# Linear attention into a sine-gated feed-forward, one core: attention outputs as four 64x64 PE tiles, w_in in natural row order, and a reordered opening

## The chip, the cores and the metric

The kernel runs on one core of one Trainium2 chip. A core has TensorE (PE, matmuls; its weight loads are PEld), VectorE (DVE), ScalarE (ACT), GpSimd (POOL) and SyncE (SP, which issues the DMAs here). All times are microseconds (us) on the device unless marked ns; less is better. The number that is compared is the median time of one execution.

## The reference

Inputs are float32. q, k and v are 8 batches x 8 heads x 576 positions x 64.

```python
q_s = softmax(q, axis=-1)            # over the 64 features of one position
k_s = softmax(k, axis=2)             # over the 576 positions
kv  = einsum('bhsd,bhse->bhde', k_s, v)      # 64x64 for each batch and head
x   = einsum('bhsd,bhde->bhse', q_s, kv)     # then (b s) rows of (h e) = 4608 x 512
h   = x @ w_in                               # 4608 x 2048
g   = h + sin(alpha * h)**2 / (alpha + 1e-9)
out = g @ w_out                              # 4608 x 512
```

## The kernel before

The order on every engine is the order in which the code is written; the framework adds the semaphores. Work falls into an attention part for each batch b (0 to 7) and a feed-forward part for each token tile t (0 to 8) of 512 tokens. Tile t needs the attention of batches up to t, so batch t+1 is worked on inside tile t.

**Attention of one batch.** `load` brings q, k and v into staging tiles (pool `stage`, six buffers that weights share). `exp_q` and `exp_k` (ACT, lines 121) write `qe` and `ke`. `norm_q` sums over features on DVE (line 149), takes the reciprocal and multiplies (line 151; from batch 2 on as one POOL instruction of 128x2304). `cast_v` (line 135, POOL) writes v as bf16 into `vb`, beside a column of ones. `kv_mm` (line 160) makes k-exp times [v, 1] in `kvp`: 36 matmuls of 64x130, two row halves in turn. `kv_norm` divides by the sum and writes two 64x64 blocks into the diagonal of a zeroed 128x128 tile `kvb`. `q_transpose` (line 186) makes three groups of six 128x128 transposes into `tp`, copied to `qT`. `attn_out` (line 195) makes eight matmuls with `kvb` as weights, 256 or 320 columns each, copied to `xT` (line 198).

**Feed-forward of one tile.** For ni = 0 to 15, `mm_h` (line 208) makes four matmuls into one of four `hp` buffers; `sine` (lines 214 to 220) takes the sine on ACT into one of three `s` buffers and squares it on ACT, POOL or DVE as a letter string says (`SQ0` in tiles 0 and 1, ACT from tile 2 on); `combine` (line 224, DVE) writes g. `mm_o` (line 228) makes g times w_out. In tiles t >= 2 the 64 `mm_o` of tile t-1 are spread between the `mm_h` by a count `want`: 20 right after ni = 0, then two or three for each ni. Tile 0's `mm_o` run as one block behind tile 0; its four results are evacuated by `evac_o` (line 233) through three `o` buffers and stored by SP.

**Where the attention stands inside a tile.** At ni = 0: exp_q, exp_k, norm_q, cast_v, then the loads of the next batch. At ni = 4: `kv_mm` and `kv_norm`; at ni = 6 to 8 the transposes; at ni = 9 to 12 `attn_out`. All of it is written ahead of that ni's sine and combine, so on DVE an evacuation of step ni stands ahead of combine(ni) and behind combine(ni-1). Batch 0 is done in the opening, batch 1 in one block between tile 0's `mm_o` and tile 1 (the middle below). All attention results in PSUM go through `ps_a`, two buffers of one bank.

**Weights.** w_in comes in four chunks of 512 columns. Its rows are ordered (x hp d), so that the two 64-row halves of an `xT` column block sit on partitions 0 to 63 and 64 to 127; each chunk is two DMAs of 64 partitions (line 108). w_out comes in four DMAs of 128 partitions (line 113). `cast_win` and `cast_wout` make bf16: win 0 and 2 on POOL, 1 and 3 on DVE, wout on POOL. In the changed kernel line numbers shift by a few; names stay.

Of the kernel before, what the change touches and what calls it, by code (L numbers as in the profile page):

```python
# [23 lines left out]
def kernel(  # L24
# [140 lines left out]
    def kv_norm(b):  # L165
        A["kvb", b] = kt = kvb[b % 2]
        kvr = small.tile([128, 2, 2], F32, name="kvr")
        for e in range(2):
            for x in range(2):
                r = slice(64 * x, 64 * x + 64)  # L170
                src = A["kvp", b][e][r, 0:260].rearrange("p (ii c) -> p ii c", ii=2)
                nc.vector.reciprocal(kvr[r, e], src[:, :, x * 65 + 64])  # L172
                nc.vector.tensor_tensor(  # L173
                    kt[r, e::2, x * 64:(x + 1) * 64],
                    src[:, :, x * 65:x * 65 + 64],
                    kvr[r, e].unsqueeze(2).to_broadcast([64, 2, D]), op=ALU.mult)

    def q_transpose(b, g, eng):
# [69 lines left out]
    for n in range(2):  # L248
        nc.vector.memset(vb[n].rearrange("p j (i c) -> p j i c", i=4)[:, :, :, D:D + 1], 1.0)
        nc.vector.memset(kvb[n], 0.0)  # L250
    tpa = ps_a.tile([128, nN], F32, name="tpa", tag="a")
    nc.tensor.transpose(tpa, alpha_rows, ident[0:nN, 0:nN])
    DVE_CP(alpha_sb, tpa)
    nc.vector.reciprocal(inva_sb, alpha_sb)

    exp_q(0)
    exp_k(0)
    norm_q(0, [nc.vector, nc.vector])
    cast_v(0, nc.gpsimd)
    for c in range(4):  # L260
        load_wout(c)
    for g in range(3):
        q_transpose(0, g, ACT_CP)
    for ii in range(2):
        kv_mm(0, ii)
    kv_norm(0)
# [7 lines left out]
    cast_win(0, nc.gpsimd.tensor_copy)  # L274
    for hp in range(4):
        attn_out(0, hp, 0, DVE_CP)
        attn_out(0, hp, 1, ACT_CP)
    cast_win(1, DVE_CP)


    load_batch(1)
    SQ0 = "APADAPADPADAPADP"
    for ni in range(nN):
        hp = mm_h(0, ni)
        if ni == 2:
            cast_win(2, nc.gpsimd.tensor_copy)
        if ni == 6:
            cast_win(3, DVE_CP)
        if ni in (7, 10, 13):
            cast_wout(ni // 3 - 2, nc.gpsimd.tensor_copy)  # L290
        combine(0, ni, hp, sine(0, ni, hp, SQ0[ni]))
    cast_wout(3, nc.gpsimd.tensor_copy)
# [13 lines left out]
    for g in range(3):
        q_transpose(1, g, ACT_CP)
    kv_mm(1, 0)
    kv_mm(1, 1)
# [80 lines left out]
```

## Time and profile before

| what | us |
|---|---|
| three timed runs | 364.56, 365.46, 366.04; median 365.46 |
| the profiled execution: its own time, and its span | 367.3, and 365.4 |
| opening, up to the first `mm_h` | 0 to 23.2 |
| tile 0, up to the first `mm_o` | 23.2 to 45.8 |
| tile 0's 64 `mm_o` | 45.8 to about 59.4 |
| middle: evacuation and batch 1's attention, up to tile 1 | 59.4 to 69.1 |
| tile 1 (with batch 2) | 69.1 to 104.5 |
| tiles 2 to 6 (with batches 3 to 7) | 104.5 to 291.5, 37.4 each |
| tiles 7 and 8, then the last `mm_o` and stores | 291.5 to 365.4 |

The sections follow from the starts of `mm_h` and `mm_o` in the timeline. The profile shows one execution. A busy share is an average over stages with different limits, so the waits are read stage by stage. In a timeline row the brackets hold the engine's idle time before the instruction and what ended it. The column PEclk is TensorE's granted clock as a share of 2.4 GHz.

### The profile page before, as it was taken

The page shows a single profiled execution, that of the slowest core. Times are in us where ns is not written, and L with a number is a line of the kernel's source. Part 1 is how long each engine was busy: PE and PEld are TensorE (multiplying, and loading weights), DVE is VectorE, ACT ScalarE, POOL GpSimd, SP SyncE. Part 2 cuts the span into 40 slices and gives each one's busy share as a digit, 9 for nine tenths or more (in the row PEclk, how much of TensorE's full clock was granted, in tenths as well). Part 3 has the DMA queues.
Part 4 walks back from the last instruction along what each step waited for, and adds up shares of the span by engine and source line. Part 5 has one row for each costly group of instructions (what it writes and reads, how often), then busy time and mean ns, then how long its engine had stood idle before and what let it go on. Part 6 is the DMA issues. An engine that isn't in the chain of part 4 may idle for free.

```text
span 365.4 us, 4429 instructions
## 1 busy us (share of the span) xinstructions
PE 302.0 (83%) x1619; PEld 145.5 (40%) x1649; DVE 210.6 (58%) x358; ACT 238.5 (65%) x332; POOL 67.1 (18%) x45
## 2 busy tenths in 40 slices
PE   0577698727795999699978998799969999999994
PEld 0432244204342454255434543454435444444441
DVE  4359673435976584658554865486547754454421
ACT  4467572593499378937893779377947777777700
POOL 0323843035125100510042003300240000000000
PEclk9999899686899899969996999699969999999998
DMA  7999972899301003901291119211101112112132
GB/s 267 273 212 282 388 275 67 285 392 392 146 0 29 11 19 69 376 33 31 57 365 54 29 35 342 99 29 31 39 20 30 29 32 56 29 31 57 29 77 68
DMA packets 22821, 46.43 MB, mean 127 GB/s; under 512 B 1792, under 2 KB 1808, under 8 KB 22800
## 3 DMA queue, kind: packets, MB, share of 16 engines
q1 hardware_dynamic: 22800, 46.15, 41.2%
q8 instruction: 13, 0.21, 0.3%
q14 instruction: 8, 0.07, 0.1%
HBM read 36.71 MB, written 9.44 MB: 126 GB/s over the span
## 4 chain that ended last, share of the span: by engine, by line
PE 61%; POOL 10%; DMA 9%; DVE 8%; ACT 6%; issue 3%; SPq 1%; POOLq 0%; DVEq 0%
PE hp L208 27%; PE op L228 27%; POOL qn L151 7%; DMA st_w<-in_moe_w_out_dram 6%; DMA st_w<-in_moe_w_in_dram 3%; DVE qs L149 3%; PE kvp L160 3%; POOL vb L135 2%; PE xp L195 2%; DVE g L224 2%; PE hp L228 2%; ACT qe L121 2%; ACT s L214 2%; ACT L121 1%; PE tp L186 1%
## 5 line engine op out<-in xcount | busy, mean ns | idle before, releaser
L208 PE MATMUL hp<-xT,win 128*128 128x512 bf16 x561 | 154.5, 402 | 7.6 <-DVE g L224 6.3
L224 DVE SCALAR_TENSOR_TENSOR g<-s,inva_sb,hp 128x512 bf16<-128x512 f32 x144 | 106.8, 746 | 86.2 <-ACT s L216 72.5
L214 ACT ACTIVATE s<-hp,alpha_sb 128x512 f32<-128x512 f32 x144 | 98.2, 684 | 77.8 <-PE hp L208 61.9
L228 PE MATMUL op<-wout,g 128*128 128x512 bf16 x529 | 139.7, 387 | 1.7 <-issue 1.0
L208 PEld LDWEIGHTS <-win 128*128 128x128 bf16 x576 | 59.2, 103 | 86.2 <-issue 27.1
L216 ACT ACTIVATE s<-s 128x512 f32<-128x512 f32 x126 | 79.3, 630 | 4.0
L228 PEld LDWEIGHTS <-g 128*128 128x128 bf16 x576 | 56.2, 99 | 62.8 <-issue 5.1
L151 POOL TENSOR_TENSOR qn<-qe,qs 128x2304 bf16<-128x2304 bf16 (+1 forms) x7 | 26.4, 3773 | 156.3 <-PE hp L208 131.5
L160 PE MATMUL kvp<-vb,ke 64*128 64x130 bf16 x288 | 16.6, 285 | 29.8 <-POOL vb L135 28.5
L149 DVE TENSOR_REDUCE qs<-qe 128x36 f32<-128x2304 bf16 (+1 forms) x10 | 20.7, 2072 | 20.3 <-ACT qe L121 20.3
L233 DVE COPY o<-op 128x512 f32<-128x512 f32 x34 | 22.9, 676 | 15.2 <-PE op L228 15.2
L160 PEld LDWEIGHTS <-ke 64*128 64x128 bf16 x288 | 13.9, 127 | 33.8 <-issue 28.3
L198 DVE CAST xT<-xp 128x256 bf16<-128x256 f32 (+1 forms) x56 | 23.0, 446 | 3.2 <-PE xp L195 3.1
L195 PE MATMUL xp<-qT,kvb 128*128 128x256 bf16 x64 | 16.5, 320 | 6.8 <-DVE kvb L173 3.4
L186 PE MATMUL tp<-identb,qn 128*128 128x128 bf16 x144 | 12.7, 230 | 10.3 <-DVE qn L151 9.4
L135 POOL CAST vb<-st_v 128x1152 bf16<-128x1152 f32 x16 | 18.8, 1199 | 10.6 <-DMA st_v<-in_v_dram 10.6
L121 ACT ACTIVATE qe<-st_q 128x1152 bf16<-128x1152 f32 x16 | 17.8, 1155 | 3.5 <-DMA st_q<-in_q_dram 3.4
L121 ACT ACTIVATE ke<-st_k 128x1152 bf16<-128x1152 f32 x16 | 17.7, 1149 | 1.9 <-DMA st_k<-in_k_dram 1.9
L186 PEld LDWEIGHTS <-qn 128*128 128x128 bf16 x144 | 10.5, 103 | 15.5 <-DVE qn L151 9.7
L172 DVE RECIPROCAL kvr<-kvp 64x2 f32<-64x2 f32 x32 | 5.4, 167 | 18.8 <-PE kvp L160 18.3
L218 POOL TENSOR_TENSOR s<-s 128x512 f32<-128x512 f32 x10 | 10.5, 1054 | 25.1 <-ACT s L214 25.1
L195 PEld LDWEIGHTS <-kvb 128*128 128x128 bf16 x64 | 6.3, 101 | 13.8 <-DVE kvb L173 4.4
(27 smaller groups left out, 90.0 us busy)
## 6 DMA issues: line engine op xcount, KB each, us to landing
out_dram<-o SPq DMA_DIRECT2D x72, 128.0 KB, 2.4
st_q<-in_q_dram SPq DMA_DIRECT2D x7, 1152.0 KB, 6.9
st_k<-in_k_dram SPq DMA_DIRECT2D x7, 1152.0 KB, 9.3
st_v<-in_v_dram SPq DMA_DIRECT2D x7, 1152.0 KB, 10.5
st_w<-in_moe_w_in_dram SPq DMA_DIRECT2D x8, 512.0 KB, 17.0
st_w<-in_moe_w_out_dram SPq DMA_DIRECT2D x4, 1024.0 KB, 20.2
st_q<-in_q_dram SPq DMA_DIRECT2D x2, 576.0 KB, 4.3
st_k<-in_k_dram SPq DMA_DIRECT2D x2, 576.0 KB, 6.8
```

The source lines that it names most:

```text
L121: nc.scalar.activation(dst[:, :, ii * 128:(ii + 1) * 128].rearrange("p j (x d) -> p x j d", x=2), src[:, ii::2], AX.Exp)
L135: eng.tensor_copy(vv[:, 2 * ii:2 * ii + 2, :, 0:D], staged["v", b][:, ii::2])
L149: nc.vector.tensor_reduce(part, src, axis=AXL.X, op=ALU.add)
L151: engs[h].tensor_tensor(dst, src, part.unsqueeze(3).to_broadcast([128, J, w, D]), op=ALU.mult)
L160: nc.tensor.matmul(kvp[e][:, ii * 130:(ii + 1) * 130], ke[r, j, ii * 128:(ii + 1) * 128], vt[r, j, ii * 130:(ii + 1) * 130], start=(j == 0 ...
L186: nc.tensor.transpose(tp[:, jj, ii], qn[:, 3 * g + jj, ii * 128:(ii + 1) * 128], identb)
L195: nc.tensor.matmul(xp[:, 0:n], kt[:, hp, :], qT[:, j0:j1, ii, e * 64:(e + 1) * 64], start=True, stop=True)
L208: nc.tensor.matmul(hp, win[:, ki, ni * 128:(ni + 1) * 128], xT[:, ki, t * MF:(t + 1) * MF], start=(ki == 0), stop=(ki == 3))
L214: nc.scalar.activation(s, hp, AX.Sin, scale=alpha_sb[:, ni:ni + 1])
L216: nc.scalar.activation(s, s, AX.Square)
L224: nc.vector.scalar_tensor_tensor(G[t][:, ni], in0=s, scalar=inva_sb[:, ni:ni + 1], in1=hp, op0=ALU.mult, op1=ALU.add)
L228: nc.tensor.matmul(acc, G[t][:, ni, j * 128:(j + 1) * 128], wout[:, ni, :], start=(ni == 0), stop=(ni == nN - 1))
```

## The change

- `attn_out` no longer multiplies with a block-diagonal 128x128 tile. `kvb` is now 64x64 blocks without zeros, and each group (ii, half) is four matmuls: row half x (heads of one parity of x) by column half e, each with 64x64 weights, into bank x of a two-bank `xp`. There are four groups of four matmuls for a batch, and four evacuations of 2x256 or 2x320 columns, in place of eight matmuls and eight evacuations. `kv_norm` is two reciprocals and two multiplies in place of four and four.
- With that, a feature row lands on its own partition in natural order, so w_in is read as (ko ki): one DMA of 128 partitions for each chunk.
- `q_transpose` makes two groups, of twelve and six transposes.
- PSUM: the opening has its own pool `ps_s`, four buffers of two banks. Behind it `ps_h`, `ps_o` and `ps_a` are opened; `ps_a` is now one buffer of two banks. `reuse_waits="tile"` makes a reused bank wait for its own last tile only.
- `cast_v` is ahead of `norm_q` from batch 2 on; in batch 0 it is half on POOL and half on DVE, in batch 1 half on DVE and half on POOL.
- Tiles 0 and 1: `combine(ni)` stands behind the sine and square of ni+1; the letter strings are new; all four `cast_win` are on POOL (ni = 1, 3, 5), two `cast_wout` at ni = 8 and 12 and two behind the tile. Tile 0's `evac_o` alternates DVE and ACT.
- In tiles t >= 1 the transposes stand at ni = 6 and 7, and the four groups of `attn_out` at ni = 8 to 11.

```diff
-    ps_a = ctx.enter_context(tc.tile_pool(name="ps_a", bufs=2, space=bass.MemoryType.PSUM))
...
-    win_v = moe_w_in.rearrange("(x hp d) n -> x d hp n", x=2, hp=4)
+    win_v = moe_w_in.rearrange("(ko ki) n -> ki ko n", ki=128)
...
-        for x in range(2):
-            nc.sync.dma_start(out=st[64 * x:64 * x + 64], in_=win_v[x][:, :, c * 512:(c + 1) * 512])
+        nc.sync.dma_start(out=st, in_=win_v[:, :, c * 512:(c + 1) * 512])
...
+        for x in range(2):
+            r = slice(64 * x, 64 * x + 64)
+            src = A["kvp", b][r, :, 0:260].rearrange("p e (ii c) -> p e ii c", ii=2)
+            nc.vector.reciprocal(kvr[r], src[:, :, :, x * 65 + 64])
+            nc.vector.tensor_tensor(kt[r], src[:, :, :, x * 65:x * 65 + 64],
+                                    kvr[r].unsqueeze(3).to_broadcast([64, 2, 2, D]), op=ALU.mult)
...
-        xp = ps_a.tile([128, 512], F32, name="xp", tag="a")
-        nc.tensor.matmul(xp[:, 0:n], kt[:, hp, :], qT[:, j0:j1, ii, e * 64:(e + 1) * 64],
-                         start=True, stop=True)
+        xp = pool.tile([128, 2, 512], F32, name="xp", tag="a")
+        for x in range(2):
+            r = slice(64 * x, 64 * x + 64)
+            for e in range(2):
+                nc.tensor.matmul(xp[64 * e:64 * e + 64, x, 0:n], kt[r, e, ii, :],
+                                 qT[r, j0:j1, ii, e * 64:(e + 1) * 64], start=True, stop=True)
...
+    with tc.tile_pool(name="ps_s", bufs=4, space=PSUM) as ps_s:
...
+        cast_v(0, [GP, V])
...
+    ps_a = ctx.enter_context(tc.tile_pool(name="ps_a", bufs=1, space=PSUM, reuse_waits="tile"))
+    SQ0 = "APADAPADAPADAPAA"
...
+        if ni in (1, 3, 5):
+            cast_win(ni // 2 + 1, POOL_CP)
+        elif ni in (8, 12):
+            cast_wout(ni // 4 - 2, POOL_CP)
+        s = sine(0, ni, hp, SQ0[ni])
+        if pend:
+            combine(0, *pend)
+        pend = (ni, hp, s)
...
+        evac_o(0, j, accs[j], ACT_CP if j % 2 else DVE_CP)
...
+    SQ1 = "PAPDPAPDPAPDPAPA"
...
-                norm_q(b, [nc.gpsimd])
-                cast_v(b, nc.gpsimd)
+                cast_v(b, [GP, GP])
+                norm_q(b, [GP])
```

The engines' own order shows three of these moves. On POOL, tiles 3 and 4 before: `qn` is the normalize of a batch, `vb_98` and `vb_99` the two buffers of v.

```order
L151 TENSOR_TENSOR qn<-qe,qs 128x2304 [waits PE_49,DVE_49,Activation_49,Pool_49]
L135 CAST vb_98<-st_v 128x2x9x64 [waits DMAHW6_49]
L135 CAST vb_98<-st_v 128x2x9x64
L151 TENSOR_TENSOR qn<-qe,qs 128x2304 [waits PE_49,DVE_49,Activation_49,Pool_49]
L135 CAST vb_99<-st_v 128x2x9x64 [waits DMAHW1_49]
L135 CAST vb_99<-st_v 128x2x9x64
```

And now, with `vb_89` and `vb_90` for the same two buffers:

```order
L131 CAST vb_89<-st_v 128x2x9x64 [waits DMAHW2_49]
L131 CAST vb_89<-st_v 128x2x9x64
L147 TENSOR_TENSOR qn<-qe,qs 128x2304 [waits PE_49,DVE_49,Activation_49,Pool_49]
L131 CAST vb_90<-st_v 128x2x9x64 [waits DMAHW5_49]
L131 CAST vb_90<-st_v 128x2x9x64
L147 TENSOR_TENSOR qn<-qe,qs 128x2304 [waits PE_49,DVE_49,Activation_49,Pool_49]
```

The casts of a batch moved from behind its normalize to ahead of it; they wait for their DMA alone.

On ACT in the middle, from batch 1's second exp on, before:

```order
L121 ACTIVATE ke<-st_k 128x2x9x64 [waits DMAHW4_49]
L121 ACTIVATE ke<-st_k 128x2x9x64
L187 COPY qT<-tp 128x768 [waits PE_49] x3
L198 CAST xT<-xp 128x320 [waits PE_49] x4
L214 ACT_TABLE_LOAD
```

And now:

```order
L117 ACTIVATE ke<-st_k 128x2x9x64
L234 COPY o<-op 128x512 [waits PE_49]
L234 COPY o<-hp 128x512 [waits DMAHW2_49,DMAHW3_49,DVE_49,PE_49]
L184 COPY qT<-tp 128x1536 [waits PE_49]
L184 COPY qT<-tp 128x768 [waits PE_49]
L199 CAST xT<-xp 128x2x320 [waits PE_49] x2
L215 ACT_TABLE_LOAD [waits PE_49]
```

Two evacuations of tile 0's result came in ahead of the copies to `qT`, and the second of them waits for two DMAs (the store that frees its `o` buffer).

On PE in tile 2, around one step of `attn_out`, before and now:

```order
L208 MATMUL hp<-xT,win 128x512
L195 LDWEIGHTS kvb_101
L195 MATMUL xp<-qT,kvb_101 128x256 [waits DVE_49]
L195 LDWEIGHTS kvb_101
L195 MATMUL xp<-qT,kvb_101 128x320 [waits DVE_49]
L228 LDWEIGHTS g
L228 MATMUL op<-wout,g 128x512
```

```order
L209 MATMUL hp<-xT,win 128x512
L196 LDWEIGHTS kvb
L196 MATMUL xp<-qT,kvb 64x256 [waits DVE_49]
L196 LDWEIGHTS kvb
L196 MATMUL xp<-qT,kvb 64x256
L196 LDWEIGHTS kvb
L196 MATMUL xp<-qT,kvb 64x256
L196 LDWEIGHTS kvb
L196 MATMUL xp<-qT,kvb 64x256
L229 LDWEIGHTS g
L229 MATMUL op<-wout,g 128x512
```

Two 128-row matmuls with a wait each became four 64x64 ones with one wait.

## Rows read from the trace of the kernel before

**Rows 1.** The page, part 1: busy us (share), instructions.

```profile
PE 302.0 (83%) x1619; PEld 145.5 (40%) x1649; DVE 210.6 (58%) x358; ACT 238.5 (65%) x332; POOL 67.1 (18%) x45
```

**Rows 2.** The chain that ended last, tile 2: start, us, what.

```profile
101.90 3.45 PE hp L208 x16
...
113.44 4.05 POOL qn L151
117.48 2.22 POOL vb L135 x2
...
124.98 0.34 PE tp L186 x6
...
130.52 0.24 PE xp L195 x2
```

**Rows 3.** Waits of tiles 2 to 6 (104.3 to 291): total, times, longest.

```profile
PE kvp L160 <- POOL vb L135: 19.6, 6, 3.9
```

**Rows 4.** PE by stretch: length, busy (instructions), granted clock, DMA share, GB/s.

```profile
151.70:155.58 3.88, 0.09 (x1) 0.84 1.02 374
155.58:161.20 5.62, 5.62 (x45) 0.50 0.08 31
291.49:346.80 55.31, 55.05 (x253) 1.00 0.17 39
```

**Rows 5.** Timeline of ACT in tile 3: start, us.

```profile
147.11 2.20 ACT L121 ACTIVATE ke<-st_k 128x1152 bf16<-128x1152 f32 x2
150.62 0.69 ACT L214 ACTIVATE s<-hp,alpha_sb 128x512 f32<-128x512 f32 x1
```

**Rows 6.** Groups by line and shape: xcount | busy us, mean ns | idle before.

```profile
L224 DVE SCALAR_TENSOR_TENSOR g<-s,inva_sb,hp 128x512 bf16<-128x512 f32 x144 | 106.8, 746 | 86.2 <-ACT s L216 72.5 <-POOL s L218 12.4
L214 ACT ACTIVATE s<-hp,alpha_sb 128x512 f32<-128x512 f32 x144 | 98.2, 684 | 77.8 <-PE hp L208 61.9 <-DVE g L224 15.0 <-PE op L228 0.4
L216 ACT ACTIVATE s<-s 128x512 f32<-128x512 f32 x126 | 79.3, 630 | 4.0
L198 DVE CAST xT<-xp 128x320 bf16<-128x320 f32 x24 | 11.5, 481 | 0.0
L187 DVE COPY qT<-tp 128x768 bf16<-128x768 bf16 x18 | 9.9, 552 | 0.3
L173 DVE TENSOR_TENSOR kvb<-kvp,kvr 64x128 bf16<-64x128 f32 x32 | 9.2, 289 | 1.1
L187 ACT COPY qT<-tp 128x768 bf16<-128x768 bf16 x6 | 4.5, 804 | 9.0 <-PE tp L186 9.0
```

**Rows 7.** DMA while q/k, w_in and w_out come in: last two columns.

```profile
9.00:11.00 2.00, 0.29 (x1) 0.10 (x1) 1.93 (x4) 1.67 (x2) 0.00 (x0) 1.00 1.06 397
...
29.00:31.00 2.00, 1.54 (x8) 0.58 (x6) 1.98 (x2) 1.59 (x3) 1.73 (x2) 1.00 1.07 214
37.00:39.00 2.00, 0.81 (x4) 0.29 (x3) 0.00 (x0) 0.52 (x1) 2.00 (x2) 1.00 1.07 393
```

**Rows 8.** Timeline of the opening and tile 0, several engines.

```profile
23.22 4.99 PE L208 MATMUL hp<-xT,win 128*128 128x512 bf16 x19 [0.22 <-issue]
...
28.54 1.89 POOL L269 CAST win<-st_w 128x2048 bf16<-128x2048 f32 x1 [0.72 <-DMA st_w<-in_moe_w_in_dram]
29.18 1.80 DVE L220 TENSOR_TENSOR s<-s 128x512 f32<-128x512 f32 x1
36.88 1.89 POOL L272 CAST wout<-st_w 128x2048 bf16<-128x2048 f32 x1 [5.01 <-DMA st_w<-in_moe_w_out_dram]
```

**Rows 9.** The chain that ended last, in the middle (59 to 70).

```profile
59.13 0.70 DVE o L233
...
60.44 2.38 DMA out_dram<-o
```

**Rows 10.** Timeline of PE in the middle and tile 1.

```profile
62.37 1.18 PE L160 MATMUL kvp<-vb,ke 64*128 64x130 bf16 x35 [0.47 <-ACT qT L187]
69.11 5.92 PE L208 MATMUL hp<-xT,win 128*128 128x512 bf16 x19 [0.22 <-issue]
...
83.92 2.27 PE L160 MATMUL kvp<-vb,ke 64*128 64x130 bf16 x36 [8.88 <-POOL vb L135]
```

More of the change, by code (lines that the diff above doesn't have):

```diff
@@ L151, in norm_q, with kv_mm @@
             engs[h].tensor_tensor(dst, src, part.unsqueeze(3).to_broadcast([128, J, w, D]), op=ALU.mult)
-    def kv_mm(b, ii):
+    def kv_mm(b, ii, pool):
         if ii == 0:
-            A["kvp", b] = [ps_a.tile([128, 512], F32, name="kvp", tag="a") for _ in range(2)]
+            A["kvp", b] = pool.tile([128, 2, 512], F32, name="kvp", tag="a")
         kvp, ke, vt = A["kvp", b], A["ke", b], vb[b % 2]
@@ L165, in kv_norm, with q_transpose @@
     def kv_norm(b):
-        A["kvb", b] = kt = kvb[b % 2]
+        A["kvb", b] = kt = att2.tile([128, 2, 2, D], BF16, name="kvb")
         kvr = small.tile([128, 2, 2], F32, name="kvr")
[L168 to L178, printed above, removed]
+        for x in range(2):
[4 more added lines that the diff above has]
+                                    kvr[r].unsqueeze(3).to_broadcast([64, 2, 2, D]), op=ALU.mult)
+    TP = ((0, 6), (6, 9))
+    def q_transpose(b, g, pool, eng):
         if g == 0:
@@ L249 @@
         nc.vector.memset(vb[n].rearrange("p j (i c) -> p j i c", i=4)[:, :, :, D:D + 1], 1.0)
[L250 to L266, printed above, removed]
     def cast_win(c, eng):
@@ L272, in cast_wout @@
         eng(wout[:, 4 * c:4 * c + 4, :], wst["o", c])
[L274 to L282, printed above, removed]
+    with tc.tile_pool(name="ps_s", bufs=4, space=PSUM) as ps_s:
+        tpa = ps_s.tile([128, nN], F32, name="tpa", tag="a")
+        nc.tensor.transpose(tpa, alpha_rows, ident[0:nN, 0:nN])
+        DVE_CP(alpha_sb, tpa)
+        nc.vector.reciprocal(inva_sb, alpha_sb)
+        exp_q(0)
+        exp_k(0)
+        norm_q(0, [V, V])
+        cast_v(0, [GP, V])
+        for c in range(4):
+            load_wout(c)
+        for g in range(2):
+            q_transpose(0, g, ps_s, ACT_CP)
+        for ii in range(2):
+            kv_mm(0, ii, ps_s)
+        kv_norm(0)
+        cast_win(0, POOL_CP)
+        for ii in range(2):
+            attn_out(0, ii, 0, ps_s, DVE_CP)
+            attn_out(0, ii, 1, ps_s, ACT_CP)
+        load_batch(1)
+    ps_h = ctx.enter_context(tc.tile_pool(name="ps_h", bufs=4, space=PSUM, reuse_waits="tile"))
+    ps_o = ctx.enter_context(tc.tile_pool(name="ps_o", bufs=2, space=PSUM, reuse_waits="tile"))
+    ps_a = ctx.enter_context(tc.tile_pool(name="ps_a", bufs=1, space=PSUM, reuse_waits="tile"))
+    SQ0 = "APADAPADAPADAPAA"
+    pend = None
     for ni in range(nN):
         hp = mm_h(0, ni)
[L285 to L292, printed above, removed]
+        if ni in (1, 3, 5):
[6 more added lines that the diff above has]
+        pend = (ni, hp, s)
+    combine(0, *pend)
+    cast_wout(2, POOL_CP)
+    cast_wout(3, POOL_CP)
     accs = [ps_o.tile([128, dm], F32, name="op", tag="o") for _ in range(2)]
@@ L299 @@
     exp_q(1)
-    norm_q(1, [nc.vector, nc.gpsimd])
+    norm_q(1, [V, GP])
     exp_k(1)
-    cast_v(1, nc.gpsimd)
+    cast_v(1, [V, GP])
     for j in range(4):
-        evac_o(0, j, accs[j], DVE_CP)
+        evac_o(0, j, accs[j], ACT_CP if j % 2 else DVE_CP)
     load_batch(2)
[L306 to L309, printed above, removed]
+    for g in range(2):
+        q_transpose(1, g, ps_a, ACT_CP)
+    kv_mm(1, 0, ps_a)
+    kv_mm(1, 1, ps_a)
     kv_norm(1)
-    for hp in range(4):
-        attn_out(1, hp, 0, DVE_CP)
-        attn_out(1, hp, 1, ACT_CP)
+    for ii in range(2):
+        attn_out(1, ii, 0, ps_a, DVE_CP)
+        attn_out(1, ii, 1, ps_a, ACT_CP)
     def o_stream(t):
@@ L328 @@
         done = 0
+        pend = None
         for ni in range(nN):
@@ L353 @@
                     done += 1
+        if pend:
+            combine(t, *pend)
         if os is not None:
```

53 lines of the change are left out of this document (30 added, 23 removed).

## The prediction

> **What bounds the kernel now.** The page comes first: PE is busy 83% of the span, more than any other engine [rows 1]. That is an average, so I go by tiles. Tiles 7 and 8, which carry no attention, take 55.31 for 256 matmuls of 512 columns, 0.216 each, at the full granted clock and with PE busy throughout [rows 4]; nothing in the change touches them, nor the 18.6 behind them. Tiles 2 to 6 take 37.4 each (from the sixteen `mm_h` that end tile 1 and begin tile 2 at 104.5 [rows 2] to 291.49 [rows 4], over five). Their PE work at full clock is: 128 matmuls, 27.66; `kv_mm` 1.2, from 35 matmuls in 1.18 [rows 10]; three groups of transposes at 0.34, 1.02; four pairs of `attn_out` at 0.24, 0.96 [rows 2]. Sum 30.84. So 6.56 of each tile is lost, and the reader should see where: `kv_mm` waits for the cast of v, 19.6 in six waits over five tiles, 3.9 a tile [rows 3]. In tile 3 PE stands from 151.70 to 155.58; behind that wait it runs 5.62 at granted clock 0.50, the lower level of 1.2 GHz, where tiles 7 and 8 run at 2.4 GHz, which costs half of it, 2.8 [rows 4]. 3.9 + 2.8 = 6.7, the whole loss. The chain says why the cast is late: POOL normalizes q for 4.05 and only then casts v for 2.22 [rows 2], though v needs no normalize.
>
> The opening and tile 0 are bound otherwise: by DMA and by POOL's order. While q, k and w_out come in at 393 to 397 GB/s, w_in, the only load on 64 partitions, comes in at 214 with the DMA engines as busy [rows 7]. The first `cast_wout` makes POOL wait 5.01 for its DMA until 36.88 [rows 8], and the squares queued behind it on POOL wait too.
>
> **The change, part by part.**
>
> *v ahead of q, tiles 2 to 6.* POOL has cast v of the next batch long before PE asks: the cast waits for its DMA alone and stands right behind the previous normalize. What is late next is `ke`: ACT finishes it at 147.11 + 2.20 = 149.31 [rows 5], 2.4 ahead of PE's arrival at 151.70 [rows 4]. The normalize no longer waits for anything new; it ends 4.05 after its reciprocal, at 154.4 in tile 3. PE would now come to the transposes near 156, so that cover is 1.6, thin but enough. The idle 3.9 goes, and with it the reason for the low clock, 2.8.
>
> *One buffer in `ps_a`.* This takes some of it back. `kvp`, two `tp` and four `xp` now follow each other through one buffer, so PE waits for each evacuation, which stands on DVE behind the combine of the step before. I walk it in tile 3. ACT resumes sines at 150.62 [rows 5], with a step each 1.24 (0.684 + 0.630, which overlap by some 0.07 [rows 6]). combine(3) ends at 155.2; `kv_norm` follows, two multiplies of twice the width of the 0.289 ones plus two reciprocals, about 1.2, so to 156.4. PE gets to the first twelve transposes at 156.0: stall 0.5 with the semaphore. combine(5) and one result copy end at 158.6; the copy of 1536 elements takes 0.95 (0.552 for 768 [rows 6], on the same slope), to 159.6. PE wants the second group at 158.7: stall 1.0. From there PE's step is 0.86 + 0.65 + 0.13, longer than ACT's, the copies of 512 and 640 columns take 0.67 and 0.79 (0.481 for 320 [rows 6]), and each ends ahead of PE's return. With 0.3 for small gaps: 1.8 a tile.
>
> *Four 64x64 tiles.* Were the four to run at once, a batch is (256 + 320) x 2 columns, 0.48 in place of 0.96. No row of before shows column halves at work together; the nearest, `kv_mm`, has two row halves in turn: 35 matmuls of 130 columns in 1.18 are 34 ns each [rows 10], where 130 columns one after the other would need 54. So two at once is shown. One end is 0.48, the other all sixteen in a row, 16 x 288 columns at 2.4 GHz, 1.92. I take 0.5, by that row.
>
> Tile: 30.84 - 0.46 + 1.8 = 32.2, a gain of 5.2; five tiles, **26.0**. Bounds: 30.4 without a stall, 34.5 with twice the stalls and half the concurrency.
>
> *Opening.* Three things shorten the way to the first `mm_h` at 23.22 [rows 8]: half of v's cast on DVE (PE starts `kv_mm` a little under 1 earlier), `kv_norm` at 1.2 (0.8 less), and four buffers for four `xp`, so that the matmuls run ahead of the copies and these alternate, two on DVE at 0.67 and two on ACT at 0.7 (0.804 for 768 [rows 6]): about 2.3, where four pairs of rounds before, each a matmul and a copy at 0.4 and 0.48, make 3.5. Together 3.0; first `mm_h` near 20.2.
>
> *Tile 0.* Before it takes 22.6. w_in in 128 partitions at 390 GB/s is four chunks of 1.05 MB at 2.7 each: they land at 16, 18.7, 21.4 and 24.1 and w_out from 26.8 on, where the first w_out cast got its data at 36.88. No POOL instruction waits for weights then. Walking ACT (1.88 for a pair of steps with one square), POOL (1.89 a cast [rows 8]) and DVE with the deferred combine, the first `mm_o` that has all four accumulators comes 17.8 after the first `mm_h`. Against that: three of the casts now run while DVE squares. In the trace, the DVE square at 29.18 took 1.80 beside a POOL cast of 28.54 to 30.43 and ended just behind it [rows 8]; three such squares add about 2.0. So tile 0 takes 19.8, 2.8 less; with the opening 5.8, of which I keep **5.5**; bounds 3 and 8. The Trainium skill (SBUF — State Buffer, Who interferes with whom) says that a DVE instruction with two SBUF inputs and a GpSimd instruction that reads SBUF exclude each other, the later one waiting in full; the 1.80 agrees, and the rule would price the move of win 1 and 3 from DVE to POOL as a loss by itself.
>
> *Middle.* This gets longer. Tile 0's fourth result needs an `o` buffer, free when the first one's store lands: 59.13 to 62.82 [rows 9], 3.7. Before, DVE took that wait, under the cover of the transposes' copies on ACT and of `kv_mm`. Now the fourth copy is on ACT, and both copies to `qT` are queued behind it; with one buffer, everything hangs on them. From the first result copy: fourth copy ends at 4.4; copy of 1536 elements, 1.45 (twice 0.804 less a start), 5.85; transposes and copy, 7.5; `kv_mm` at low clock, 2.27 [rows 10], since PE has then been idle over 4 with 3.9 enough in tile 3, 9.9; `kv_norm` 11.35; four rounds of matmul, semaphore and copy at 1.3: 16.5. Before: 69.11 - 59.13 = 9.98 [rows 9, 10]. A loss of **6.2**, bounds 4 (full clock) and 8.
>
> *Tile 1.* Before 35.4. Two costs go: `kv_mm` waited 8.88 for the cast [rows 10], with POOL squares queued behind both. Now casts end 5.6 into the tile, the normalize at 12.9, `kv_mm` goes behind the fifth `mm_h` at 10.3; after that DVE sets the pace, 1.4 to 2.1 a step for ni 6 to 11 (combine 0.746 [rows 6], a copy, and a square in some). The walk ends at 29.7: a gain of **5.7**, bounds 3 and 8.
>
> Sum: 26.0 + 5.5 - 6.2 + 5.7 = 31.0. The profiled execution took 367.3 around a span of 365.4: 336.3. The median of the runs lies 1.84 lower (365.46): **334.5**.
>
> **Rivals.**
>
> A. No buffer stalls: PE's returns fall behind the evacuations everywhere, tile 30.4. 9.0 more: 325.5. For it: DVE idles 86 ahead of combines [rows 6]; against: the walk's queue at ni = 6.
>
> B. The clock stays low for some 5.6 in each tile all the same, since the stalls around ni = 6 replace the long one: +2.8 x 5, 348.5. Against: one stall of 1.0, where 3.9 preceded the fall.
>
> C. The 64x64 matmuls run one after the other. Tiles 1 to 6: +1.44 each, 8.6; opening and middle at half clock: four groups of 0.85 to 1.07 in place of a quarter, 2.9 each, 5.8. Total +14.4: 349. For it: nothing in the trace has four tiles. The Trainium skill (TensorEngine Tiling (Array Packing), Key Properties) says that a change of tiling mode drains TensorE, and eight such changes a batch are new; no row here prices one.
>
> D. w_in's rate is not its 64 partitions but its 2 KB pieces of 8 KB rows: the last chunk lands near 32 as before, and the tile 0 gain shrinks by 4: 338.5. Against: w_out has 2 KB pieces too, at 393.
>
> E. Slower: each of the seven fills of the one buffer waits for a combine that waits for ACT, a chain of sine, square, combine and copy, 0.684 + 0.630 + 0.746 + 0.73 = 2.8 [rows 6] against PE's step of 1.64, 1.15 a fill, 8.1 a tile; with the clock low for 10 of it, +5: 43.5 a tile, 30.5 more than now, less 5.0 from the other parts: 391. It decides where a fill costs more than (37.4 + 1.0 - 30.4) / 7 = 1.1. It needs ACT to stay a step behind; its 1.24 is below 1.64.
>
> **How the numbers follow.** Forecast 0.62, A 0.12, B 0.07, C 0.10, D 0.04, E 0.05. The bounds of the terms put the forecast's own range at about 325 to 344; to leave no more than 2 in 10 out it reaches A below and B and C above: 322 to 350. About 0.5% is what a measurement of this kernel can tell from no change. Faster 0.94 (all but E and a remainder), same 0.02, slower 0.04.
>
> **What would show it.** Right: the wait of `kv_mm` for the cast is gone from tiles 2 to 6, granted clock 1.00 from the fourth `mm_h` on, tiles near 32; PE's transposes waiting about 1 for DVE once a tile; w_in near 390 GB/s; the first `mm_o` near 40; on ACT a wait of about 3 for a store in the middle, tile 1 starting about 16 behind the first result copy. Wrong: `kv_mm` waiting for `ke` or a DMA of v, `attn_out` at over 0.3 a group at full clock, or a wait of PE for DVE at each ni from 8 to 11.

## The result, and the profile after

The changed kernel takes 339.85 us (median of 4 runs, 338.83 to 341.35), the kernel before on the same chip 365.54 (364.56 to 366.04): a ratio of 0.930, 95% interval 0.926 to 0.935. The time lies in the predicted range; the predicted value, 334.5, is 5.35 too low. The profiled execution took 340.48 around a span of 338.7.

The spans differ by 26.7, and the section boundaries, read in both traces as in the table ahead, give this account (one boundary of that table is put right: by the timeline, tile 2's first `mm_h` starts at 104.33 before, not at 104.5; it starts at 100.29 after):

| section | before | after | measured | predicted |
|---|---|---|---|---|
| up to the first `mm_o` | 45.76 | 40.51 | -5.25 | -5.5 |
| first `mm_o` to tile 0's first result copy | 13.37 | 13.75 | +0.4 | 0 |
| from there to tile 1's first `mm_h` | 9.98 | 15.12 | +5.1 | +6.2 |
| tile 1 | 35.2 | 30.9 | -4.3 | -5.7 |
| tiles 2 to 6 | 187.2 | 164.6 | -22.6 | -26.0 |
| tiles 7 and 8 and the end | 73.9 | 73.8 | -0.1 | 0 |

The page, part 1 (busy us, share, instructions), for [rows 1]; then PE's waits in tiles 2 to 6 (total, times, longest), for [rows 3]:

```profile
PE 291.6 (86%) x1713; PEld 134.9 (40%) x1713; DVE 200.6 (59%) x286; ACT 237.5 (70%) x328; POOL 71.7 (21%) x47
```

```profile
PE tp L183 <- DVE kvb L168: 4.1, 5, 1.1
PE tp L183 <- DVE qT L184: 2.3, 5, 0.5
```

The wait of `kv_mm` for the cast, 19.6 in [rows 3], is gone. What stands in its place is two short waits a tile, both for DVE, and both for the one buffer of `ps_a`. PE by stretch (length, busy, granted clock, DMA share, GB/s), a stretch of tile 3 and tiles 7 and 8, for [rows 4]:

```profile
133.00:166.00 33.00, 31.79 (x200) 1.00 0.43 140
264.86:320.20 55.34, 55.34 (x259) 1.00 0.17 39
```

The granted clock, 0.50 behind the long wait before, is 1.00. Tiles 7 and 8 have not moved (55.31 before).

The timeline of PE in tile 3 (start, length, instruction, idle before it in brackets) shows the rest:

```profile
129.81 1.03 PE L209 MATMUL hp<-xT,win 128*128 128x512 bf16 x4
130.67 0.81 PE L229 MATMUL op<-wout,g 128*128 128x512 bf16 x3
131.32 1.03 PE L209 MATMUL hp<-xT,win 128*128 128x512 bf16 x4
...
142.97 1.03 PE L209 MATMUL hp<-xT,win 128*128 128x512 bf16 x4
143.93 1.20 PE L156 MATMUL kvp<-vb,ke 64*128 64x130 bf16 x36
145.06 0.82 PE L229 MATMUL op<-wout,g 128*128 128x512 bf16 x3
...
147.01 1.03 PE L209 MATMUL hp<-xT,win 128*128 128x512 bf16 x4
148.78 0.83 PE L183 MATMUL tp<-identb,qn 128*128 128x128 bf16 x12 [0.74 <-DVE kvb L168]
149.45 0.81 PE L229 MATMUL op<-wout,g 128*128 128x512 bf16 x3
150.10 1.03 PE L209 MATMUL hp<-xT,win 128*128 128x512 bf16 x4
151.59 0.49 PE L183 MATMUL tp<-identb,qn 128*128 128x128 bf16 x6 [0.47 <-DVE qT L184]
151.92 0.81 PE L229 MATMUL op<-wout,g 128*128 128x512 bf16 x3
152.57 1.03 PE L209 MATMUL hp<-xT,win 128*128 128x512 bf16 x4
153.53 0.30 PE L196 MATMUL xp<-qT,kvb 64*64 64x256 bf16 x4
153.76 0.82 PE L229 MATMUL op<-wout,g 128*128 128x512 bf16 x3
154.42 1.03 PE L209 MATMUL hp<-xT,win 128*128 128x512 bf16 x4
```

Read it by starts, because the ends of matmuls are modelled. Four `mm_h` take 0.86 from start to start (129.81 to 130.67), and a step with three `mm_o` takes 1.51 (129.81 to 131.32). Against that:

- The first transposes start 1.77 after their `mm_h` (147.01 to 148.78), so 0.91 is lost, though the bracket says 0.74; the second 1.49 after theirs, so 0.63 is lost. Together 1.54 a tile.
- A step with a 64x64 group takes 1.85 (152.57 to 154.42), 0.34 more than the plain one. 0.10 of that is ahead of the group, which starts 0.96 after its `mm_h`, not 0.86.

`kv_mm` starts at 143.93 with no wait, and the next three at 176.74, 209.54 and 242.35: a tile is 32.81 in the steady state. The same distance before is 37.53 (193.10, 230.63, 268.17, each with a wait of 3.86 for the cast). So the gain is 4.7 a tile in the steady state, where 5.2 was predicted; averaged over the five tiles by the table it is 4.5, because between the `kv_mm` of tiles 2 and 3 the distance went from 36.94 to 33.19 only.

In the middle, ACT's timeline:

```profile
58.06 0.58 ACT L234 COPY o<-hp 128x512 f32<-128x512 f32 x1 [3.00 <-DMA out_dram<-o]
58.54 1.45 ACT L184 COPY qT<-tp 128x1536 bf16<-128x1536 bf16 x1
60.87 0.80 ACT L184 COPY qT<-tp 128x768 bf16<-128x768 bf16 x1 [0.89 <-PE tp L183]
```

and PE's:

```profile
54.70 0.83 PE L183 MATMUL tp<-identb,qn 128*128 128x128 bf16 x12
60.04 0.80 PE L183 MATMUL tp<-identb,qn 128*128 128x128 bf16 x6 [4.50 <-ACT qT L184]
61.72 2.13 PE L156 MATMUL kvp<-vb,ke 64*128 64x130 bf16 x36 [0.89 <-ACT qT L184]
```

ACT waits 3.00 for the store that frees its `o` buffer, both copies to `qT` stand behind it, PE waits 4.50, and `kv_mm` then takes 2.13 instead of the 1.20 of tile 3.

The DMA rate while w_in comes in (last column GB/s; the columns ahead are length, then PE, PEld, DVE, ACT and POOL busy, clock, DMA share), for [rows 7]:

```profile
21.00:23.00 2.00, 2.00 (x6) 0.76 (x5) 0.75 (x1) 1.83 (x3) 0.04 (x1) 0.50 1.05 387
```

It is 387 GB/s where it was 214. Last, in tile 0, two of the three squares on DVE, then POOL, then PE, for [rows 8]:

```profile
25.79 2.43 DVE L221 TENSOR_TENSOR s<-s 128x512 f32<-128x512 f32 x1 [1.00 <-ACT s L215]
...
31.94 1.21 DVE L221 TENSOR_TENSOR s<-s 128x512 f32<-128x512 f32 x1 [0.39 <-ACT s L215]
```

```profile
23.95 3.73 POOL L254 CAST win<-st_w 128x2048 bf16<-128x2048 f32 x2
...
30.71 1.89 POOL L257 CAST wout<-st_w 128x2048 bf16<-128x2048 f32 x1
```

```profile
28.92 3.71 PE L209 MATMUL hp<-xT,win 128*128 128x512 bf16 x16 [2.54 <-DVE g L225]
33.86 3.70 PE L209 MATMUL hp<-xT,win 128*128 128x512 bf16 x16 [1.23 <-DVE g L225]
```

### The profile page after: what moved, and what is told of

It reads as the page before. It is cut to its first block, busy times and chain, and to the rows that moved or that the text cites. A ratio compares the mean times of both kernels' runs of the same rounds, so it can differ in the third digit from the quotient of the medians.

```text
span 338.7 us, 4528 instructions
## 1 busy us (share of the span) xinstructions
PE 291.6 (86%) x1713; PEld 134.9 (40%) x1713; DVE 200.6 (59%) x286; ACT 237.5 (70%) x328; POOL 71.7 (21%) x47
## 4 chain that ended last, share of the span: by engine, by line
PE 49%; ACT 21%; DVE 18%; issue 6%; POOL 2%; DMA 2%; SPq 0%; ACTq 0%; POOLq 0%
PE op L229 22%; PE hp L209 20%; ACT s L215 7%; DVE g L225 7%; ACT ke L117 3%; ACT qe L117 3%; ACT L215 2%; ACT L117 2%; ACT s L217 2%; PE xp L196 2%; DVE kvb L168 2%; PE hp L229 2%; DVE s L221 2%; DVE qT L184 2%; PE tp L183 2%
## 5 line engine op out<-in xcount | busy, mean ns | idle before, releaser
L209 PE MATMUL hp<-xT,win 128*128 128x512 bf16 x576 | 150.5, 389 | 12.4 <-DVE g L225 11.4
L209 PEld LDWEIGHTS <-win 128*128 128x128 bf16 x576 | 56.8, 100 | 84.5 <-issue 21.4
L229 PEld LDWEIGHTS <-g 128*128 128x128 bf16 x576 | 53.8, 98 | 63.4 <-issue 0.5
L147 POOL TENSOR_TENSOR qn<-qe,qs 128x2304 bf16<-128x2304 bf16 (+1 forms) x7 | 26.7, 3817 | 115.2 <-PE hp L209 100.7
L199 DVE CAST xT<-xp 128x512 bf16<-128x512 f32 (+1 forms) x28 | 20.8, 745 | 5.5 <-PE xp L196 5.5
L219 POOL TENSOR_TENSOR s<-s 128x512 f32<-128x512 f32 x12 | 12.9, 1076 | 39.4 <-ACT s L215 39.4
L183 PEld LDWEIGHTS <-qn 128*128 128x128 bf16 x144 | 9.8, 104 | 26.7 <-issue 16.3
L131 POOL CAST vb<-st_v 128x1152 bf16<-128x1152 f32 x14 | 16.9, 1236 | 15.2 <-DMA st_v<-in_v_dram 15.2
L196 PE MATMUL xp<-qT,kvb 64*64 64x256 bf16 (+1 forms) x128 | 10.4, 320 | 5.4 <-DVE kvb L168 2.5
L156 PE MATMUL kvp<-vb,ke 64*128 64x130 bf16 x288 | 12.4, 252 | 0.9 <-ACT qT L184 0.9
L156 PEld LDWEIGHTS <-ke 64*128 64x128 bf16 x288 | 10.8, 112 | 4.2 <-ACT s L215 3.0
L215 ACT ACT_TABLE_LOAD x8 | 10.3, 1283 | 1.7 <-PE hp L209 1.6
L117 ACT ACT_TABLE_LOAD x8 | 10.3, 1283 | 0.9 <-PEq L392 0.7
## 6 DMA issues: line engine op xcount, KB each, us to landing
st_w<-in_moe_w_in_dram SPq DMA_DIRECT2D x4, 1024.0 KB, 13.6
```

The source lines that it names most:

```text
L117: nc.scalar.activation(dst[:, :, ii * 128:(ii + 1) * 128].rearrange("p j (x d) -> p x j d", x=2), src[:, ii::2], AX.Exp)
L147: engs[h].tensor_tensor(dst, src, part.unsqueeze(3).to_broadcast([128, J, w, D]), op=ALU.mult)
L156: nc.tensor.matmul(kvp[:, e, ii * 130:(ii + 1) * 130], ke[r, j, ii * 128:(ii + 1) * 128], vt[r, j, ii * 130:(ii + 1) * 130], start=(j == 0 ...
L183: nc.tensor.transpose(tp[:, h, 2 * jj + ii], qn[:, j, ii * 128:(ii + 1) * 128], identb)
L199: eng(xT[:, ii::2, c0:c0 + n], xp[:, :, 0:n])
L209: nc.tensor.matmul(hp, win[:, ki, ni * 128:(ni + 1) * 128], xT[:, ki, t * MF:(t + 1) * MF], start=(ki == 0), stop=(ki == 3))
```

## The experiments

My theory: the gain is the cast of v ahead of the normalize and nothing else in tiles 2 to 6; the rest of the change costs time there (stalls for the one buffer, and the 64x64 groups) and earns in the opening about what it loses in the middle. The rivals: the other parts bring much of the gain by themselves; the 64x64 matmuls don't run four at once; w_in's rate has to do with its order of rows. Each time is set against the kernel before on the same chip, whose median was 366.98 (e1 to e4), 366.56 (e5 to e8) and 365.99 (e9), beside 365.54 where the changed kernel was timed, so a microsecond between two groups of runs says nothing; tile lengths, read in the traces, are finer.

### e1: the cast behind the normalize again

```diff
-                cast_v(b, [GP, GP])
                 norm_q(b, [GP])
+                cast_v(b, [GP, GP])
```

> The changed kernel with one part undone: from batch 2 on the casts of v stand behind the normalize on POOL again. Theory 1 (the cast's wait and the low clock behind it were the loss of tiles 2 to 6): in tile 3 of the changed kernel POOL starts its normalize near 142.4, so the casts would end near 148.7 and kv_mm, which runs at 143.9, waits 4.8; the granted clock falls to 0.50 for some 5.6 behind it, 2.8 lost; the stalls of 1.3 at the transposes go, since DVE catches up meanwhile. +6.3 a tile, five tiles, and +4 to 6 in tile 1: about 375. Rival 2 (most of the gain came from the loads of w_in, the opening and the spread of work, and PE would now have other work to cover the cast): under 350.

Measured: 365.41 (8 runs), ratio 0.9985, interval 0.994 to 1.003. All of the gain is gone with this one part. Two `kv_mm` in the timeline of PE:

```profile
190.92 0.78 PE L156 MATMUL kvp<-vb,ke 64*128 64x130 bf16 x18 [3.86 <-POOL vb L131]
...
228.37 0.69 PE L156 MATMUL kvp<-vb,ke 64*128 64x130 bf16 x18 [3.86 <-POOL vb L131]
```

Each row is the first half of a `kv_mm`. The wait of 3.86 is back to the hundredth, and a tile is 37.45 (190.92 to 228.37). The granted clock drops too, to 0.57 in a stretch from 153.55 to 157.55. The stalls for the buffer nearly vanish here, as expected: in the 3.86 DVE catches up, and PE's transposes wait 0.8 in four waits, not 6.4 in ten. The costs of the change hide behind the wait that it removes. It was not as slow as the theory had it (about 375), because the wait is 3.9 and not 4.8, the lower clock lasts some 3.4 in a tile (a mean of 0.57 over 4.0) and not 5.6, so that a tile loses 4.6 and not 6.3; and from the middle's transposes to the first `mm_o` of tile 2 it takes 2.4 more (53.87 to 102.69, against 54.70 to 101.15), not 4 to 6.

### e2: the kernel before, with the cast ahead alone

```diff
-                norm_q(b, [nc.gpsimd])
                 cast_v(b, nc.gpsimd)
+                norm_q(b, [nc.gpsimd])
```

> The kernel before with one part alone: from batch 2 on cast_v stands ahead of norm_q on POOL. Theory 1: tiles 2 to 6 go from 37.4 to about 31.7 (their PE work of 30.84 and some 0.8 of waits at the transposes, with two buffers of one bank and the 128-row attention matmuls kept), tile 1 loses 4: about 332, so that this one edit is worth more than the whole change. Rival 2 (the other parts carry much of the gain): 340 or more.

Measured: 335.86, ratio 0.914, interval 0.907 to 0.921. This one move of a line is faster than the whole change, 0.930. PE in tile 3:

```profile
144.67 1.20 PE L160 MATMUL kvp<-vb,ke 64*128 64x130 bf16 x36
...
147.75 1.03 PE L208 MATMUL hp<-xT,win 128*128 128x512 bf16 x4
149.24 0.50 PE L186 MATMUL tp<-identb,qn 128*128 128x128 bf16 x6 [0.46 <-DVE kvb L173]
```

The next `kv_mm` starts at 176.17: a tile is 31.50, 1.31 shorter than in the changed kernel. There is one stall, 0.63 by starts (147.75 to 149.24, less 0.86), in place of 1.54, and the pairs of 128-row matmuls in place of the 64x64 groups. This settles where the rest of the change stands in tiles 2 to 6: on the loss side. The time is above the 332 expected, though the tiles are as expected (31.50, against 31.7): tile 1 takes 34.2 (68.51 to 102.72) and so gains 1.0, not 4, with PE waiting 4.71 for a cast and 4.63 for a combine in it.

### e3: w_in in its natural order, but in two DMAs of 64 partitions

```diff
-        nc.sync.dma_start(out=st, in_=win_v[:, :, c * 512:(c + 1) * 512])
+        for x in range(2):
+            nc.sync.dma_start(out=st[64 * x:64 * x + 64], in_=win_v[64 * x:64 * x + 64, :, c * 512:(c + 1) * 512])
```

> The changed kernel with each w_in chunk, still in natural row order, loaded as two DMAs of 64 partitions in place of one of 128. Theory 1 (the 64 partitions set the rate): about 214 GB/s while w_in comes in, its last chunk some 8 later, tile 0 waits on POOL for weights, +4 to +6. Rival 2 (the row order set the rate): 385 GB/s as in the changed kernel, no difference in time.

Measured: 346.82, ratio 0.945, interval 0.940 to 0.950. The same two microseconds as above, and POOL:

```profile
21.00:23.00 2.00, 2.00 (x6) 0.69 (x5) 0.00 (x0) 1.11 (x3) 0.00 (x0) 0.50 1.06 215
```

```profile
34.18 1.89 POOL L255 CAST win<-st_w 128x2048 bf16<-128x2048 f32 x1 [3.20 <-DMA st_w<-in_moe_w_in_dram]
```

The rate is 215 GB/s with the DMA engines just as busy (1.06), with the rows in natural order and pieces of the same length. The number of DMAs is not the reason either: q and k of batch 0 come in two DMAs each, on 128 partitions, and move 397 GB/s [rows 7]. What is left is the 64 partitions. The last cast of w_in starts at 34.18 and the first `mm_o` at 47.62 instead of 40.51. The Trainium skill (SBUF — State Buffer, Door 1: The DMA port swizzle) says that partitions 0 to 63 cover only half of the ports by which DMA reaches SBUF; 215 against 387 agrees.

### e4: the same DMAs and buffers, with block-diagonal 128x128 matmuls

The rows of w_in are in the order of before, as the 128x128 products need it.

```diff
-        for x in range(2):
-            r = slice(64 * x, 64 * x + 64)
-            for e in range(2):
-                nc.tensor.matmul(xp[64 * e:64 * e + 64, x, 0:n], kt[r, e, ii, :],
-                                 qT[r, j0:j1, ii, e * 64:(e + 1) * 64], start=True, stop=True)
+        for e in range(2):
+            nc.tensor.matmul(xp[:, e, 0:n], kt[:, e, ii, :],
+                             qT[:, j0:j1, ii, e * 64:(e + 1) * 64], start=True, stop=True)
```

> As e3_win_halves in its DMAs (64 partitions, w_in rows in the order of before), but attn_out multiplies with block-diagonal 128x128 weights: two 128-row matmuls of 256 or 320 columns for a group in place of four 64x64 ones, with the same pools, positions and copies. It is to be compared with e3_win_halves. Theory 1 (a group of four 64x64 tiles costs PE 0.34 in all, against 0.24 for the pair): tiles 1 to 6 shorter by 0.4 each, 2 to 3 less than e3_win_halves. Rival 2 (the four run at once and the extra time at them is a wait that block weights would have too): the same as e3_win_halves, or slower.

Measured: 345.05, ratio 0.940, interval 0.934 to 0.946; 1.8 less than e3, to which it is to be held. PE in its tile 3:

```profile
159.88 1.03 PE L209 MATMUL hp<-xT,win 128*128 128x512 bf16 x4
160.74 0.38 PE L196 MATMUL xp<-qT,kvb 128*128 128x256 bf16 x2
160.96 0.81 PE L229 MATMUL op<-wout,g 128*128 128x512 bf16 x3
161.61 1.03 PE L209 MATMUL hp<-xT,win 128*128 128x512 bf16 x4
```

The step takes 1.73 (159.88 to 161.61), 0.22 more than a plain one; with 64x64 tiles it was 0.34 more. The matmul starts 0.86 after its `mm_h`, without the 0.10. Tiles are 32.38 long (183.62, 216.00, 248.38), 0.43 shorter than in the changed kernel, with the same stalls (6.4 in ten waits). So the 64x64 products cost 0.43 a tile here; half the columns do not pay for it.

### e5: each group of four 64x64 matmuls issued twice

```diff
-        for x in range(2):
+        for x in (0, 1, 0, 1):
```

> The changed kernel with every group of four 64x64 matmuls issued twice in a row into the same xp (start and stop set each time, so the result is that of the second). The second four need no change of array tiling. Theory 1 (four at once, and the extra 0.1 a group is the change to and from the tiling): a second group adds one stream of 256 or 320 columns, 0.11 to 0.13, 0.5 a batch. Rival 2 (two at once): 0.21 to 0.27 more a group, 1.0 a batch. Rival 3 (one after the other): 0.43 to 0.53 more a group, 1.9 a batch. In time +3, +6 or +12 over seven batches, less what hides.

Each product is computed a second time into the same place. Measured: 343.71, ratio 0.9365, interval 0.933 to 0.940.

```profile
154.38 1.03 PE L209 MATMUL hp<-xT,win 128*128 128x512 bf16 x4
155.34 0.41 PE L196 MATMUL xp<-qT,kvb 64*64 64x256 bf16 x8
155.68 0.82 PE L229 MATMUL op<-wout,g 128*128 128x512 bf16 x3
156.34 1.03 PE L209 MATMUL hp<-xT,win 128*128 128x512 bf16 x4
```

The step takes 1.96 (154.38 to 156.34), 0.11 more than with one group: 256 columns at 2.4 GHz are 0.107. Four more 64x64 matmuls cost what the columns of one of them cost. The four do run side by side, as the prediction had it. But then the first four cost 0.11 of the 0.34, and 0.23 is a price that is paid once, for coming and going, whether four matmuls run inside or eight. The weight loads, in the changed kernel and in e4, show part of it:

```profile
153.52 0.11 PEld L196 LDWEIGHTS <-kvb 64*64 64x64 bf16 x4 [0.42 <-issue]
```

```profile
160.53 0.31 PEld L196 LDWEIGHTS <-kvb 128*128 128x128 bf16 x2
```

In e4 the load starts 0.21 ahead of its matmul (160.74), while the matmul before still runs; for a 64x64 group it starts only 0.01 ahead (153.53). The four loads overlap, 0.11 for all four. Tiles are 33.32 long (179.04, 212.35, 245.67), 0.51 more than without the second issue; four groups by columns make 0.48. By the columns, one after the other would have cost 1.9 a tile, two at once 1.0.

### e6: four `o` buffers

```diff
-    opool = ctx.enter_context(tc.tile_pool(name="opool", bufs=3))
+    opool = ctx.enter_context(tc.tile_pool(name="opool", bufs=4))
```

> The changed kernel with four o buffers in place of three, so that tile 0's fourth result on ACT needs no store to land. Theory 1 (ACT's wait of 3.00 for a store holds the copies to qT and all behind them): the middle is 3.0 shorter, 4 if PE's idle time ahead of kv_mm falls enough for the clock to stay: 335.5 to 337. Rival 2 (the chain of single-buffer rounds is bound by something else, POOL's half of the normalize or of v's cast): no difference.

Measured: 336.21, ratio 0.916, interval 0.912 to 0.919. PE in the middle:

```profile
55.73 0.83 PE L183 MATMUL tp<-identb,qn 128*128 128x128 bf16 x12
58.09 0.49 PE L183 MATMUL tp<-identb,qn 128*128 128x128 bf16 x6 [1.53 <-ACT qT L184]
59.47 1.20 PE L156 MATMUL kvp<-vb,ke 64*128 64x130 bf16 x36 [0.89 <-ACT qT L184]
```

The wait for the store is gone; PE waits 1.53 and not 4.50, and `kv_mm` takes 1.20 and not 2.13. From the transposes to tile 1's first `mm_h` (66.11) are 10.4, where it was 14.7 (54.70 to 69.38). Of the 4.3, 3.0 is the wait itself and about 1.0 the clock of `kv_mm`.

### e7: no squares on DVE in tile 0

```diff
-    SQ0 = "APADAPADAPADAPAA"
+    SQ0 = "APAAAPAAAPAAAPAA"
```

> The changed kernel with tile 0's three DVE squares made on ACT. Theory 1 (a DVE square beside a POOL cast waits for it, 2.43, 1.21 and 1.21 in place of 0.68, and PE stands 2.54, 1.23 and 1.23 behind them): PE's waits shrink, ACT takes 1.9 more: 1 to 3 less. Rival 2 (ACT is what binds tile 0): 1 to 2 more.

Measured: 337.60, ratio 0.921, interval 0.917 to 0.924. PE's waits in tile 0:

```profile
25.20 3.61 PE L209 MATMUL hp<-xT,win 128*128 128x512 bf16 x16 [0.43 <-DVE g L225]
29.86 3.61 PE L209 MATMUL hp<-xT,win 128*128 128x512 bf16 x16 [1.05 <-DVE g L225]
```

With a third of 0.30 these stand where 2.54, 1.23 and 1.23 stood. The transposes of the middle start at 51.37 instead of 54.70, although ACT has three squares more to do. That start scatters: in the five traces with the squares on DVE whose code is the same up to there (the changed kernel, e1, e5, e6 and e8) it lies between 53.87 and 55.73, and in the two without them (e7 and e9) at 51.37 and 51.69. So the squares on DVE make it 2.2 to 4.4 later, 3.1 on average; the medians give 2.25 (339.85 to 337.60), from two groups of runs.

### e8: the attention of tiles 1 to 7 one step later and further apart

```diff
-                elif ni in (6, 7):
-                    q_transpose(b, ni - 6, ps_a, DVE_CP)
-                elif 8 <= ni < 12:
-                    attn_out(b, (ni - 8) // 2, ni % 2, ps_a, DVE_CP)
+                elif ni in (7, 9):
+                    q_transpose(b, (ni - 7) // 2, ps_a, DVE_CP)
+                elif 10 <= ni < 14:
+                    attn_out(b, (ni - 10) // 2, ni % 2, ps_a, DVE_CP)
```

> The changed kernel with the transposes at ni = 7 and 9 and the four groups of attn_out at ni = 10 to 13, in tiles 1 to 6, in place of 6, 7 and 8 to 11. Theory 1 (PE's two waits for DVE at the transposes, 0.8 and 0.5 a tile, come from the one buffer and the copies queued behind combines; a step later DVE has caught up): tiles 2 to 6 shorter by 1.0 to 1.3 each, 334 to 335. Rival 2 (the waits move along with the transposes): no difference.

Measured: 331.80, ratio 0.904, interval 0.901 to 0.907, more than expected.

```profile
145.98 1.03 PE L209 MATMUL hp<-xT,win 128*128 128x512 bf16 x4
146.84 0.83 PE L183 MATMUL tp<-identb,qn 128*128 128x128 bf16 x12
...
149.67 1.03 PE L209 MATMUL hp<-xT,win 128*128 128x512 bf16 x4
150.53 0.50 PE L183 MATMUL tp<-identb,qn 128*128 128x128 bf16 x6
```

Both groups of transposes now start 0.86 after their `mm_h`: no stall is left, and from 105 to 260 PE has no wait at all. Tiles are 31.28 long (172.66, 203.94, 235.22), 1.53 less: all of the 1.54 read above by starts, where the waits as listed, 6.4 over five tiles, would give 1.28. What is left of a tile is PE's own work: 27.66 for 128 matmuls, 1.23 for `kv_mm` (143.93 to 145.06, and 0.10 ahead of it), 1.0 for the transposes and 1.42 for the groups (0.34 and 0.37, twice) make 31.3.

### e9: e6, e7 and e8 together

The three diffs above, in one kernel.

> The changed kernel with three of the edits already measured alone, together: four o buffers, no DVE squares in tile 0, and the attention of tiles 1 to 7 one step later and further apart. If the three act in different places (the middle, tile 0, tiles 2 to 6), their gains add: 339.85 - 3.6 - 2.25 - 8.05 = about 326; the period from kv_mm to kv_mm stays 31.28 as with the later positions alone, the middle is as with four o buffers, tile 0 as without DVE squares. Rival: the gains overlap, because ACT, which takes the squares of tile 0 over, ends tile 0 later and so the result copies of the middle too: then 328 to 330.

Measured: 326.29 (326.07 to 326.65), ratio 0.891, interval 0.886 to 0.897. By the medians the three gains add up, 13.6 where 13.9 was the sum, though these come from different groups of runs. In the trace each is found in its own place: tile 31.28 (136.09, 167.37, 198.64), PE's wait in the middle 1.53, the middle's transposes at 51.69. But from these to the first `mm_o` of tile 2 it takes 43.5 (to 95.22), where e6 alone took 41.1 (55.73 to 96.85), so some 2.4 of e6's gain is not kept; why, no run takes apart. It is 4% faster than the changed kernel (0.891 against 0.930). In its tiles 2 to 6 PE has no stall left, so what could still be won there is PE's own work, the price of the 64x64 groups above all.

## Why the prediction was right, and where it missed

**What bounds the kernel: right.** The wait for the cast and the low clock behind it were the whole loss of tiles 2 to 6; e1 brings back the wait and, for a shorter time, the low clock, and with them 4.6 a tile; e2 takes both away alone. The granted clock came back with the wait, as the sum had it (B falls: 1.00 in the row of tile 3). `ke` was early enough, and the normalize too: no wait for `qn` or `ke` in tiles 2 to 6.

**The stalls of the one buffer: near in sum, not in their parts.** 1.8 a tile was predicted (0.5, 1.0 and 0.3 for small gaps); 0.91 and 0.63 came, 1.54. The place and the mechanism are as walked, an evacuation on DVE behind the combine of the step before; DVE was on time (the combine ahead of `kv_norm` ends 3.5 after the start of `kv_mm`, in the walk and in the trace, 143.93 to 147.44), but PE came to the first transposes 3.94 after it, not 4.3. A falls here, and e8 shows that it was a matter of two numbers in the code: without stalls a tile is 31.28, not the 30.4 of A, and the difference is the next point.

**Four 64x64 tiles: the step that failed.** The prediction took 0.5 for a batch where it was 0.96, by the row of `kv_mm` that shows two row halves at once. It measures 1.42. That row supports two at once, which is 0.96; four at once was a guess, and e5 shows that it was a lucky one. What was missing is a price for each visit: 0.34 and 0.37 a group, of which 0.11 and 0.13 are columns and 0.23 is fixed. 0.92 more a tile, less 0.26 for the stalls, turns 32.2 into 32.86; 32.81 was measured. It is also the prediction's own sign of being wrong, `attn_out` at over 0.3 a group. `kv_mm` pays the same price, unnoticed: in tile 3 after the change it adds 1.23 to its step (142.97 to 145.06, less 0.86), where 36 matmuls of 130 columns, two at once, are 0.98 at 2.4 GHz; 0.25 is left. The 1.18 of [rows 10] did not show it: a length ends with the modelled end of the last matmul (one alone, at 61.67 in the middle, is listed with 0.23, though its 130 columns take 0.05), and no `kv_mm` of before ran at full clock between two matmuls without a wait. The Trainium skill (TensorEngine Tiling (Array Packing), Key Properties) says that changing the tiling mode drains TensorE, and the prediction put that rule with rival C. The runs agree with the rule, and not with C's serial matmuls: the start of a group moves back by 0.10 at each change from 128x128, for `kv_mm` as for `xp`, and not for `xp` in e4, where the shape stays. That the 0.23 is this drain is my reading; a weight load that is not hidden at the change would look the same, and what a change costs by itself, without matmuls, was not run.

**Opening and tile 0: right in sum, by luck.** 5.25 came of 5.5, because two misses cancel. The first `mm_h` is at 18.97, with the rest of them from 19.57, where 20.2 was predicted; tile 0 takes 21 to 21.5 and not 19.8. The three DVE squares took 2.43, 1.21 and 1.21, together 2.6 more than three that run free at 0.75 (one such stands in e8's trace, and there POOL's two casts took 4.19, not 3.73), where 2.0 was predicted, and PE stood 5.0 behind them (2.54, 1.23 and 1.23). The first square began at 25.79, with the second of POOL's two casts, and ended at 28.22, just behind the cast's end at 27.68. That is the row of before [rows 8] again. e7 takes the squares away and gains some 3 there. D falls with e3: the 64 partitions set w_in's rate, and to read it in 128 is worth 7.1 up to the first `mm_o`, more than the 5.25 that all parts of the opening gained together.

**Middle and tile 1: right in mechanism and, together, in size.** The wait for the store (3.00, predicted 3), the copies behind it and `kv_mm` at half clock came as walked: from the first result copy at 54.26 the fourth copy ends after 4.4, the second copy to `qT` after 7.4 (walk: 7.5), `kv_mm` after 9.6 (9.9). e6 shows the cause, and that the clock was lost by the wait alone. The last step is a matter of where one cuts: the first `mm_h` of tile 1 starts at 69.38, ahead of the last copy, and the others at 70.24, behind it. From there, as the walk counted, the middle is 16.0 (16.5 predicted) and tile 1 is 30.05 (29.7). Tile 1 still did not go as walked: PE waits 5.02 for a combine while ACT does batch 2's exps, so `kv_mm` starts 13.3 into the tile and not 10.3, and takes 2.13. Why the end came out nearly right no run takes apart.

**The sum.** 334.5 was 5.35 too low. Of that 3.4 are in tiles 2 to 6, 0.3 in the middle and tile 1 together, 0.25 ahead of the first `mm_o` and 0.4 behind it; and 1.2 come from the step from execution to median: this execution lay 0.63 above its median, where the one of before lay 1.84 above its own. 0.1 less around the span and rounding make the rest. E is out: ACT stayed ahead, and no step from ni = 8 to 11 waits in tile 3.

## What to carry to other kernels

When a long wait goes, everything that it had covered comes to light: so test each part of a change against the kernel without that wait, as in e2, where one moved line beats the whole change. Here a group of matmuls in another tile shape than its neighbours cost a fixed 0.23 for each visit, so count visits and not columns alone, and give a visit enough work. With one buffer between two engines, space its uses so far apart that the evacuation ends ahead of the next one: two step numbers were worth 8 here.
